# Moving the low-part differences of MoE1 from GpSimd to VectorE in an attention, MoE1, MoE2 kernel

## The chip, the cores and the metric

The kernel runs on one core of a Trainium2 chip. The metric is device time in microseconds (us), smaller is better. Engine names in the profile: PE is TensorE, PEld its weight load, DVE is VectorE, ACT is ScalarE, POOL is GpSimd, SP is SyncE, whose queue carries most loads. Each engine takes its own instructions in the order in which the program wrote them.

## The reference, cut to what matters

```
x = causal_attention(q, k, v)                    # 2 x 12 heads, 448 positions, head size 64
x -> 896 tokens x 768                            # heads laid side by side
h = x @ w_in                                     # 768 -> 2048
g = h * sigmoid(1.702 * h)
y = g @ w_out                                    # 2048 -> 768           (this is MoE1)
e = argmax(y @ w_gate); MoE2: relu(y @ w1[e]) @ w2[e], scaled by two gates
```

The weights w_in and w_out of MoE1 arrive as 64-bit floats; everything else is 32-bit.

## The kernel before, in words

**Split matmuls.** A 32-bit operand that is to be multiplied precisely is held as two numbers that TensorE takes at its fast rate: a high part (the value cast to the type `F32R` by ScalarE) and a low part (value minus high part). A product then takes three matmuls: high by high, high by low, low by high. So each weight and each activation costs a cast on ScalarE and then a subtraction that must wait for the cast.

**The stages.** Attention runs first (to about 138 us in the trace). Then L1 of MoE1 (x by w_in and the sigmoid gate, to 258.5 us), L2 of MoE1 in two passes (256 of the 768 output columns for seven token tiles, called B, to about 318 us, then the other 512, called A, to about 404 us), and then MoE2, expert by expert, to the end.

**Weights of MoE1, a stream.** `Stream` holds 48 weight tiles of 128x512 in the order of their use: 24 of w_in, 8 of w_out for part B and 16 for part A. Each is loaded by SyncE into a raw buffer and worked on in three steps, and `st.pump(n)` carries out n steps at the place in the program where it is called. Step one (L219, L221) and the first half of step two (L224) are VectorE's and turn 64-bit words into 32-bit ones; the second half of step two is ScalarE's cast into the slot (L226); step three is the subtraction (L228). A slot is one of 19 places in a ring, freed when its last matmul is issued, and the temporary 32-bit tile has two buffers.

**L1.** For each f of 16 blocks of 128 output features, the program issues six groups of matmuls (kk = 0 to 5), six matmuls in a group (two token groups times three products, L438). After each group it calls `st.pump(1)`, or `st.pump(2)` from f = 12 to f = 14, and nothing in f = 15. So two weights are converted in each f, and up to four in f = 12. The pumps in attention's stage have worked on eight weights but for the last step of the eighth, which falls in f = 0; so from f = 1 to f = 11 the six steps of an f are, in program order: step 1, 2, 3 of one weight, then 1, 2, 3 of the next. Behind them stand the four gate pieces of the block: a sigmoid by ScalarE (L536) and a product by VectorE (L537) each. The result of f sits in two banks of PSUM until the products have read it. Odd blocks take their banks from a set of four, even blocks from a set of three; so the second bank of an even block f is the bank that the first half of block f - 2 used, and its first matmul waits until the first two gate products of f - 2 are done. (PSUM tiles `ph0` and `ph4`, L431 to L433.)

**The first gate pieces of L2.** `gsplit(u)` (L496 to L509) casts a piece of g of 128x512 (ScalarE, L506) and subtracts (L508). 28 pieces serve pass B and 28 pass A. They are made three ahead of use and stand in four buffers, so that the cast of piece u + 3 waits for the matmuls of piece u - 1. For the 18 pieces listed in `GP` the subtraction is GpSimd's, for the other 38 VectorE's.

**L2, pass B.** A token tile t takes 16 values of kk, three matmuls each. At kk = 0, 4, 8 and 12 it calls `gsplit`, at kk = 5 it transposes the y of the tile before on TensorE and copies it out on VectorE (L618), at kk = 11 it multiplies that copy by the gate weights (L628), and after each kk it pumps `R2[t]` steps: 0.3 for t = 1, 2, 3 and 5, less for the others (0.1, 0.15, 0.2). TensorE's order is the program's order, so a copy L618 that is late holds every matmul behind L628.

Of the kernel before, what the change touches and what calls it, by code (L numbers as in the profile page):

```python
# [9 lines left out]
F32 = mybir.dt.float32  # L10
# [97 lines left out]
def kernel(ctx, tc, q, k, v, w_in, w_out, w_gate, w_og, w1, w2, out):  # L108
    nc = tc.nc
# [25 lines left out]
    CUT = 5  # L135
    NOV = 6
    XK = (11, 12, 13)
    GP = (4, 5, 7, 8, 10, 11, 13, 14, 16, 17, 19, 20, 22, 23, 25, 26, 27, 29)
    R1, R1B = 1, 2
    R2 = (0.1, 0.3, 0.3, 0.3, 0.15, 0.3, 0.2)  # L140
    R3 = (1.2, 1.2, 1.2, 1.2, 1.2, 1.2, 1.2)
# [17 lines left out]
    with tc.manual_schedule():  # L159
# [43 lines left out]
        def raw_tile(where, shape, dt):  # L203
            if where == "raw":
                return raws.tile(shape, dt, name="raw", tag="raw", bufs=RAW)
            return ringA.tile(shape, dt, name="rawA", tag=f"slotA{where}")

        def add64(keys, src, two=False, ring="A"):
            def load(where):
                raw = raw_tile(where, [128, 512], I64)  # L210
                nc.sync.dma_start(raw.rearrange("p (a n) -> p a n", a=2) if two else raw, src)
                return raw

            def work(keys, raw):
                slot = st.slots[keys[0]] = ring_slot(keys[0])
                r = raw.bitcast(U32).rearrange("p (n two) -> p n two", two=2)
                w = raws.tile([128, 512], F32, name="w32", tag="w32", bufs=2)
                wu = w.bitcast(U32)
                nc.vector.tensor_scalar(wu, r[:, :, 1], 3, 0x3FFFFFF8,  # L219
                                        op0=ALU.logical_shift_left, op1=ALU.bitwise_and)  # L220
                nc.vector.scalar_tensor_tensor(wu, r[:, :, 1], 0xC0000000, wu,  # L221
                                               op0=ALU.bitwise_and, op1=ALU.bitwise_or)
                yield
                nc.vector.scalar_tensor_tensor(wu, r[:, :, 0], 29, wu,  # L224
                                               op0=ALU.logical_shift_right, op1=ALU.bitwise_or)
                nc.scalar.copy(slot[:, 0], w)  # L226
                yield
                nc.gpsimd.tensor_sub(slot[:, 1], w, slot[:, 0].bitcast(F32))  # L228

            st.add(keys, ring, load, work)  # L230

# [2 lines left out]
        def ring_slot(key):  # L234
            ring, place = st.home[key]
            if ring == "A":
                return ringA.tile([128, 2, 512], F32R, name="slotA", tag=f"slotA{place}")
            return xr_p[0].tile([128, 2, 512], F32R, name="slotX", tag=f"slotX{place}")
# [83 lines left out]
        eng = {"D": nc.vector, "P": nc.gpsimd}  # L322
# [136 lines left out]
        for s in range(len(steps) + LAG + AV_AT[-1]):  # L459
# [12 lines left out]
            for c in range(NKC):  # L472
                u = s - LAG - (NQ - 1) - AV_AT[c]
# [22 lines left out]
        def gsplit(u):  # L496
            gnext[0] = u + 1
            if u >= 8 * TT:
                return
            t, qt = u % (4 * TT) // 4, u % 4  # L500
            if u < 2:
                gs = raws.tile([128, 2, GU, 128], F32R, name="gs0", tag="raw", bufs=RAW)
            else:
                gs = ggp.tile([128, 2, GU, 128], F32R, name="gs", tag="gs", bufs=4)
            src = g[t // 2 * 2][:, t % 2, GU * qt:GU * qt + GU, :]
            nc.scalar.copy(gs[:, 0], src)  # L506
            eng = nc.gpsimd if u in GP else nc.vector
            eng.tensor_sub(gs[:, 1], src, gs[:, 0].bitcast(F32))  # L508
            gsp[u] = gs  # L509

        for fq in range(4):
            for fc in range(4):
# [20 lines left out]
                for t0, nt in GT:  # L533
                    gv = g[t0][:, :, f, :]
                    pv = ph_t[f][t0 // 4].rearrange("q (t n) -> q t n", n=128)[:, t0 % 4:t0 % 4 + nt]
                    nc.scalar.activation(gv, pv, AF.Sigmoid, scale=1.702)  # L536
                    nc.vector.tensor_mul(gv, pv, gv)  # L537
                    if f == 15 and t0 == 0:
                        for u in range(2, 4):
                            gsplit(u)  # L540
                if fq == 3 and fc == 2:
                    assert st.nraw + 2 <= RAW
                    st.raws = RAW - 2
                    gsplit(0)
                    gsplit(1)
# [466 lines left out]
```

## Time and profile before

| what | value |
|---|---|
| time, median of 3 runs | 646.16 us (644.27 to 646.68) |
| the profiled execution's own time | 647.17 us |
| its span | 645.4 us |
| PE busy | 609.5 us, 94% of the span |
| DVE busy | 471.6 us, 73% |
| ACT busy | 373.6 us, 58% |
| POOL busy | 202.0 us, 31% |

The span is what the trace covers; the own time of that execution is 1.8 us more. Busy times are sums over instructions. An engine that is mostly busy over the whole run can still be idle for a long time in one stage, so the stages have to be looked at one by one.

### The profile page before, as it was taken

What the parts mean: (1) busy time and instruction counts of PE and PEld (TensorE: products, weight loads), DVE (VectorE), ACT (ScalarE), POOL (GpSimd) and SP (SyncE); (2) the same over time, 40 slices, a digit from 0 to 9 for tenths busy, and PEclk for the clock granted to TensorE, in tenths of its full rate; (3) what the DMA queues carried; (4) which work ended last, traced back from release to release, by engine and by line L of the source; (5) the groups of instructions that cost most, each with busy time, mean ns of one, the idle gap of its engine ahead of it and who ended that gap; (6) DMA issues with size and microseconds to landing.
All of it is one profiled execution on the core that took longest, in us unless ns stands there. A gap on an engine that the chain in (4) does not pass through costs nothing. (4 is left out here: it accounts for less than half of the span.)

```text
span 645.4 us, 10420 instructions
## 1 busy us (share of the span) xinstructions
PE 609.5 (94%) x3494; PEld 469.3 (73%) x3494; DVE 471.6 (73%) x890; ACT 373.6 (58%) x729; POOL 202.0 (31%) x291
## 2 busy tenths in 40 slices
PE   8999999999999979878999999959999999999995
PEld 4444544478888868867777777647888888888884
DVE  2766666637777777877855447757998888988896
ACT  4777777633333333434333224547888888888885
POOL 3344444416333342567511001241361110111110
PEclk8999999999999998999899999989999999999998
DMA  6735353115444453322393502446999999999960
GB/s 143 230 79 140 74 122 89 36 34 137 131 131 134 136 167 118 117 71 63 102 315 110 164 17 74 147 142 216 353 337 364 372 306 384 382 382 382 383 213 20
DMA packets 93146, 118.06 MB, mean 183 GB/s; under 512 B 40206, under 2 KB 53406, under 8 KB 93088
## 3 DMA queue, kind: packets, MB, share of 16 engines
q1 hardware_dynamic: 88560, 109.05, 52.2%
q0 software_dynamic: 2512, 5.54, 2.4%
q10 hardware_dynamic: 2016, 2.75, 1.2%
q8 instruction: 30, 0.49, 0.3%
q14 instruction: 28, 0.23, 0.1%
HBM read 114.10 MB, written 7.54 MB: 188 GB/s over the span
## 5 line engine op out<-in xcount | busy, mean ns | idle before, releaser
L576 PE MATMUL py<-slotA,gs 128*128 128x256 f32 (+1 forms) x609 | 115.1, 343 | 1.3 <-POOL gs L508 1.3
L576 PEld LDWEIGHTS py<-slotA,gs 128*128 128x128 f32 x609 | 93.5, 196 | 14.0 <-issue 2.6
L438 PE MATMUL ph<-xhi,slotA 128*128 128x512 f32 (+1 forms) x384 | 97.0, 372 | 4.7 <-DVE g L537 4.7
L228 POOL TENSOR_TENSOR slotA<-w,slotA 128x512 fp32r<-128x512 f32 x45 | 62.0, 1378 | 81.7 <-ACT slotA L226 81.6
L438 PEld LDWEIGHTS ph<-xhi,slotA 128*128 128x128 f32 x384 | 70.4, 190 | 15.2 <-issue 5.7
L226 ACT CAST slotA<-w 128x512 fp32r<-128x512 f32 x45 | 27.9, 620 | 89.2 <-DVE w L224 89.2
L301 DVE TENSOR_TENSOR ent<-wraw,ent 128x1024 fp32r<-128x1024 f32 x48 | 58.0, 1221 | 4.8 <-ACT ent L300 4.8
L367 PE MATMUL sc<-kz,qT 128*64 128x64 f32 (+6 forms) x336 | 56.3, 412 | 0.9 <-ACT kz L357 0.9
L380 DVE TENSOR_REDUCE nmax<-sc 128x1 f32<-128x64 f32 (+6 forms) x84 | 35.5, 422 | 29.6 <-PE sc L369 29.2
L391 POOL TENSOR_SCALAR P<-P,rc 128x64 f32<-128x64 f32 (+2 forms) x72 | 36.5, 508 | 65.4 <-DVE rc L390 56.3
L382 ACT ACTIVATE P<-sc,nmax 128x64 f32<-128x64 f32 (+6 forms) x84 | 40.0, 476 | 28.0 <-DVE nmax L380 15.9
L438 PE MATMUL ph<-xlo,slotA 128*128 128x512 f32 x192 | 56.0, 372 | 0.0
L508 DVE TENSOR_TENSOR gs<-g,gs 128x512 fp32r<-128x512 f32 x38 | 31.5, 836 | 31.9 <-ACT gs L506 31.8
L876 PE MATMUL ps_h<-ent,xh 128*128 128x512 f32 x192 | 53.8, 402 | 0.0
L224 DVE SCALAR_TENSOR_TENSOR w<-raw,w 128x512 uint32<-128x512 uint32 x46 | 51.9, 1129 | 1.2
L300 ACT CAST ent<-wraw 128x1024 fp32r<-128x1024 f32 x48 | 49.8, 1049 | 0.4 <-ACT y L598 0.4
L537 DVE TENSOR_TENSOR g<-ph,g 128x256 f32<-128x256 f32 x64 | 23.6, 389 | 29.6 <-ACT g L536 29.6
L506 ACT CAST gs<-g 128x512 fp32r<-128x512 f32 x56 | 33.1, 616 | 14.6 <-PE py L576 9.0
L876 PEld LDWEIGHTS ps_h<-ent,xh 128*128 128x128 f32 x192 | 35.0, 188 | 7.3
L301 DVE TENSOR_TENSOR ent<-wrb,ent 128x1024 fp32r<-128x1024 f32 x30 | 36.3, 1222 | 4.7 <-ACT ent L300 4.2
L221 DVE SCALAR_TENSOR_TENSOR w<-raw,w 128x512 uint32<-128x512 uint32 x46 | 38.0, 827 | 1.6
L438 PEld LDWEIGHTS ph<-xlo,slotA 128*128 128x128 f32 x192 | 35.5, 191 | 4.8
(190 smaller groups left out, 1202.4 us busy)
## 6 DMA issues: line engine op xcount, KB each, us to landing
wraw<-in_moe_w_dram SPq DMA_DIRECT2D x66, 512.0 KB, 7.7
wrb<-in_moe_w_dram SPq DMA_DIRECT2D x48, 512.0 KB, 9.0
wr<-in_moe_w_dram SPq DMA_DIRECT2D x30, 512.0 KB, 6.3
raw<-in_moe_w_in_dram SPq DMA_DIRECT2D x24, 512.0 KB, 4.5
raw<-in_moe_w_out_dram SPq DMA_DIRECT2D x22, 512.0 KB, 3.6
qraw<-in_q_dram SPq DMA_DIRECT2D x24, 112.0 KB, 2.9
kraw<-in_k_dram SPq DMA_DIRECT2D x24, 112.0 KB, 3.0
vraw<-in_v_dram SPq DMA_DIRECT2D x24, 96.0 KB, 2.6
```

Of the source, the lines that this page charges most:

```text
L221: nc.vector.scalar_tensor_tensor(wu, r[:, :, 1], 0xC0000000, wu, op0=ALU.bitwise_and, op1=ALU.bitwise_or)
L224: nc.vector.scalar_tensor_tensor(wu, r[:, :, 0], 29, wu, op0=ALU.logical_shift_right, op1=ALU.bitwise_or)
L228: nc.gpsimd.tensor_sub(slot[:, 1], w, slot[:, 0].bitcast(F32))
L300: nc.scalar.copy(hi, raw)
L301: nc.vector.tensor_sub(lo, raw, hi.bitcast(F32))
L367: nc.tensor.matmul(sc[64 * h:64 * h + 64, :n], qT[:, j * QB:(j + 1) * QB], kT[:, h, :n], start=True, stop=False)
L380: nc.vector.tensor_reduce(nm, sc[:, :n], axis=AX.X, op=ALU.max, negate=True)
L382: nc.scalar.activation(Pb[j][:, :n], sc[:, :n], AF.Exp, bias=nm, scale=1.0, accum_out=sm)
L391: eng[NORM_ENG[j]].tensor_scalar(Pb[j][:, :n], Pb[j][:, :n], rc, 1.0, op0=ALU.mult, op1=ALU.mult)
L438: nc.tensor.matmul(p[:, 0:128 * nt], wt, xt[:, kk, 128 * t0:128 * (t0 + nt)], start=kk == 0 and n == 0, stop=kk == KD - 1 and n == 2)
L576: nc.tensor.matmul(py[:, :n], gt[:, kk % 4], wt, start=kk == 0 and m == 0, stop=kk == KF - 1 and m == 2)
L876: nc.tensor.matmul(hps[hf], xh[:, k0 + n], wt[:, n], start=k0 + n == 0 and m == 0, stop=False)
```

## The change

Both subtractions that GpSimd did in MoE1 go to VectorE: step three of each weight (48 instructions, L228), and the 18 pieces of g in `GP` (L508). Their places in the program order stay the same.

```diff
-    GP = (4, 5, 7, 8, 10, 11, 13, 14, 16, 17, 19, 20, 22, 23, 25, 26, 27, 29)
...
                 nc.scalar.copy(slot[:, 0], w)
                 yield
-                nc.gpsimd.tensor_sub(slot[:, 1], w, slot[:, 0].bitcast(F32))
+                nc.vector.tensor_sub(slot[:, 1], w, slot[:, 0].bitcast(F32))
...
             nc.scalar.copy(gs[:, 0], src)
-            eng = nc.gpsimd if u in GP else nc.vector
-            eng.tensor_sub(gs[:, 1], src, gs[:, 0].bitcast(F32))
+            nc.vector.tensor_sub(gs[:, 1], src, gs[:, 0].bitcast(F32))
```

## Rows read from the trace of the kernel before

**Rows 1.** The page's busy times: us (share of the span) xinstructions.
```profile
PE 609.5 (94%) x3494; PEld 469.3 (73%) x3494; DVE 471.6 (73%) x890; ACT 373.6 (58%) x729; POOL 202.0 (31%) x291
```

**Rows 2.** Stretches: us, PE, PEld, DVE, ACT, POOL busy (count), PEclk, DMA share, GB/s.
```profile
75.00:100.00 25.00, 25.00 (x188) 12.08 (x184) 16.64 (x59) 18.18 (x57) 10.35 (x21) 1.00 0.45 107
140.50:222.50 82.00, 82.00 (x398) 72.18 (x397) 60.38 (x106) 27.29 (x65) 32.45 (x64) 1.00 0.44 130
258.50:318.70 60.20, 50.11 (x380) 46.74 (x380) 47.61 (x54) 24.94 (x50) 40.70 (x28) 0.94 0.28 87
294.70:301.20 6.50, 6.50 (x56) 6.17 (x54) 5.04 (x7) 3.17 (x6) 3.98 (x4) 1.00 0.35 101
```

**Rows 3.** Timeline of PE in L1: start us, us, instruction [idle before <-releaser].
```profile
230.58 0.99 PE L438 MATMUL ph<-xhi,slotA 128*128 128x512 f32 x4
231.82 0.99 PE L438 MATMUL ph<-xhi,slotA 128*128 128x512 f32 x4
...
242.27 0.64 PE L438 MATMUL ph<-xhi,slotA 128*128 128x384 f32 x1 [4.68 <-DVE g L537]
```

**Rows 4.** Timeline of DVE over one block f of L1.
```profile
182.90 0.42 DVE L219 TENSOR_SCALAR w<-raw 128x512 uint32<-128x512 uint32 x1
183.35 0.69 DVE L221 SCALAR_TENSOR_TENSOR w<-raw,w 128x512 uint32<-128x512 uint32 x1
184.08 0.69 DVE L224 SCALAR_TENSOR_TENSOR w<-raw,w 128x512 uint32<-128x512 uint32 x1
184.69 0.42 DVE L219 TENSOR_SCALAR w<-raw 128x512 uint32<-128x512 uint32 x1
...
185.87 1.66 DVE L224 SCALAR_TENSOR_TENSOR w<-raw,w 128x512 uint32<-128x512 uint32 x1
188.50 0.42 DVE L537 TENSOR_TENSOR g<-ph,g 128x256 f32<-128x256 f32 x1 [0.97 <-ACT g L536]
...
190.68 0.42 DVE L219 TENSOR_SCALAR w<-raw 128x512 uint32<-128x512 uint32 x1
```

**Rows 5.** Timeline of ACT in the same block.
```profile
184.80 0.62 ACT L226 CAST slotA<-w 128x512 fp32r<-128x512 f32 x1 [2.15 <-DVE w L224]
...
188.09 0.38 ACT L536 ACTIVATE g<-ph 128x256 f32<-128x256 f32 x1
```

**Rows 6.** Timeline of POOL in the same block.
```profile
185.50 1.48 POOL L228 TENSOR_TENSOR slotA<-w,slotA 128x512 fp32r<-128x512 f32 x1 [3.73 <-ACT slotA L226]
```

**Rows 7.** Instructions of L228, then of L508: duration ns min/median/max, first and last start.
```profile
L228 POOL TENSOR_TENSOR slotA<-w,slotA x45: 1261/1293/1747, 33.0 to 325.3; 128x512 fp32r<-128x512 f32 x45
...
L508 DVE TENSOR_TENSOR gs<-g,gs x38: 673/692/1726, 256.2 to 393.2; 128x512 fp32r<-128x512 f32 x38
```

**Rows 8.** Timeline of DVE: the first gate product of f = 0, 11, 12.
```profile
142.24 0.42 DVE L537 TENSOR_TENSOR g<-ph,g 128x256 f32<-128x256 f32 x1 [3.04 <-ACT g L536]
...
227.51 0.42 DVE L537 TENSOR_TENSOR g<-ph,g 128x256 f32<-128x256 f32 x1 [1.02 <-ACT g L536]
...
240.83 0.42 DVE L537 TENSOR_TENSOR g<-ph,g 128x256 f32<-128x256 f32 x1 [1.02 <-ACT g L536]
```

**Rows 9.** What PE waited for from 260 to 330 us: us, times, longest.
```profile
PE ps_lT L628 <- DVE yT L618: 7.9, 4, 3.7
PE py L576 <- POOL gs L508: 1.3, 1, 1.3
```

**Rows 10.** DVE's groups by form from 260 to 330 us: busy us, mean ns | idle before.
```profile
L508 DVE TENSOR_TENSOR gs<-g,gs 128x512 fp32r<-128x512 f32 x15 | 15.7, 1061 | 12.6 <-ACT gs L506 12.5
L224 DVE SCALAR_TENSOR_TENSOR w<-raw,w 128x512 uint32<-128x512 uint32 x9 | 11.9, 1323 | 0.2
L221 DVE SCALAR_TENSOR_TENSOR w<-raw,w 128x512 uint32<-128x512 uint32 x9 | 11.1, 1237 | 0.3
...
L618 DVE COPY yT<-ps_yT 128x256 f32<-128x256 f32 x7 | 2.9, 414 | 0.0
```

**Rows 11.** Timeline of DVE in pass B: a piece of g behind a weight's cast.
```profile
267.10 0.69 DVE L508 TENSOR_TENSOR gs<-g,gs 128x512 fp32r<-128x512 f32 x1 [1.26 <-ACT gs L506]
```

## The prediction, made before the changed kernel was run

> **What bounds the kernel now.** I read the page's busy times first [rows 1]: PE is busy for 94% of the span, so at most some 36 us of it are gaps, and a change of two other engines acts through those gaps or not at all. Next the busy times by stretch [rows 2]. In attention PE has no gap while DVE works 16.64 of 25 us. In L1 (140.5 to 222.5) PE is again busy throughout, DVE for 60.4 of 82 us. Pass B of L2 is the stage with holes: PE 50.1 of 60.2 us, at a granted clock of 0.94, against a tile without stalls, which takes 6.5 us.
>
> Then the timelines. They show that L1's full PE row hides a debt. A group of six matmuls takes 1.24 us [rows 3], so PE needs 6 x 1.24 = 7.44 us for a block f. DVE's round for the same block takes 190.68 - 182.90 = 7.78 us [rows 4], because DVE and ACT answer each other without slack in it. DVE falls behind by a third of a us in each block; PSUM covers that up to f = 14, whose second bank waits 4.68 us for the gate products of f = 12 [rows 3, 8]. So in L1 the chain DVE - ACT - DVE is already the slower one. In pass B PE's waits are 7.9 us for DVE's copy of y, and 1.3 us for POOL's pieces of g [rows 9].
>
> **The change, part by part: L1.** The subtraction takes POOL 1.29 us. On DVE the same shape, done there already for g, takes 0.69 us [rows 7], and DVE's next instruction begins 0.61 us after the start of one of 0.69 [rows 4]. What matters is that the subtraction now stands in DVE's own queue behind ACT's cast. Behind it in that queue are the next weight's L219, L221 and L224, and after the second weight the gate products, which free PSUM for PE. Step by step for one weight [rows 4, 5]: L219 to L221 0.45, L221 to L224 0.73, L224 itself 0.69, to the cast 0.03 (184.77 to 184.80), the cast 0.62, to the subtraction 0.03 (an ACT to DVE step is 0.03 at 188.47 to 188.50), the subtraction 0.61: together 3.16 us. Two weights take 6.32 us. Today they take 188.50 - 182.90 = 5.60. The gate pieces after them stay at 190.68 - 188.50 = 2.18 us: the first sigmoid, at 188.09, is ready before DVE is free in the new order too. The round becomes 8.50 us against PE's 7.44.
>
> A gain is already in that sum. Today the second L224 takes 1.66 us and the first 0.69 [rows 4], because POOL's subtraction runs from 185.50 to 186.98 [rows 6] and L224 ends 0.55 us after it; that 0.97 us goes away. So in DVE's own time a block grows by only 2 x 0.61 - 0.97 = 0.25 us. The rest is waiting: 2 x 0.68 for the casts, less the 0.97 that DVE waits today ahead of the gate products, 0.39, and 0.08 of overlap that is lost where an instruction is waited for to its end.
>
> [...]
>
> Where it ends. The first gate product of f = 0 stays at 142.24; that of f = 11 comes at 142.24 + 11 x 8.50 = 235.7 instead of 227.51 [rows 8]. In f = 12 four weights stand between: 2.18 + 4 x 3.16 = 14.8 instead of 13.3, so f = 12's comes at 250.6 instead of 240.83. PE's matmul follows 1.44 us later (240.83 to 242.27), at 252.0: **9.7 us late**. The debt is paid in parts, because even blocks wait for the products of f - 2: about 1.7 us ahead of f = 8 (PE there at 192.9, released at 142.24 + 6 x 8.50 + 1.44 = 194.7), 2.1 each ahead of f = 10 and 12, and 8.5 ahead of f = 14. From there PE has two blocks to do, and DVE's work of f = 13 (three weights, 9.5 us) and f = 14 ends before them. Bounds: if the casts were always done when DVE comes, 11 x 0.25 - 0.5 (f = 12: 4 x 0.61 less three stretched L224) = +2.3; with POOL's step from the cast of 0.08 (185.42 to 185.50) instead of 0.03, 26 x 0.05 more, +11.0. I take 9.7: the steps are read from one and the same queue.
>
> **Pass B.** DVE gets 29 more subtractions (11 weights, nine of them in rows 10 and two from other buffers, and 18 pieces of g), and its own instructions get shorter: L224 and L221 now average 1.32 and 1.24 us here and L508 1.06 [rows 10], against 0.69 where POOL is silent. A tile with rate 0.3 (four of seven) then holds 4 pieces x 0.61, 1.6 weights x (0.45 + 0.73 + 0.61 + 0.61), and two copies, some 0.5 (0.41 for the larger [rows 10]): 6.8 us. A piece of g that comes right behind an L224 waits for two casts on ACT, 1.26 us today [rows 11]; that should meet four weights in five, 1.3 a tile: 1.6 us. So 8.4 us a tile, for PE too, since the copy of y is in that queue. The three others hold 0.5 to 1.1 weights, 4.2 to 5.5 us, and run at PE's 6.5 us. 4 x 8.4 + 3 x 6.5 = 53.1, and with the first matmuls of pass A that the stretch contains and an uneven start some 55.5 instead of 60.2: **4.7 us gained**. Bounds: all that is lost there today, 60.2 - 7 x 6.5 = 14.7 us gained; or DVE's 29 x 0.69 = 20.0 us more with only its 12.6 idle us [rows 10] to take them, 7.4 us lost. I stay nearer to the first kind because the row 1.66 against 0.69 says that most of what DVE gives here is time that it lost.
>
> **Attention** takes eight subtractions. They are emitted a pump after the cast, and DVE is idle for 8 of 25 us under a PE without gaps [rows 2]: nothing. Uncovered they would be 8 x 0.69 = 5.5 us; below nothing there is no room, as PE has no gap. The constants on POOL and pass A, whose pieces are DVE's today, lie beside other work. The loads follow freed buffers, so they move with PE and pay nothing back later.
>
> **Sum.** 647.17 (this execution's own time, 645.4 of it span) + 9.7 - 4.7 = 652.2. The median of the runs is 1.0 lower. I give 652, on the upper side, because longer gaps in L1 may lower the clock once more as those of pass B do (0.94).
>
> **The rivals.**
> *It cancels.* L1 as above, but pass B gains 8 to 10 because without POOL its copies of y are never late. For it: 7.9 of PE's waits there end with that copy [rows 9]. Against it: DVE's 6.8 us in a heavy tile exceed PE's 6.5 even without a wait. 646 to 649.
> *Faster, because DVE is no longer stretched.* If DVE came to the subtraction after the cast was done (the third steps standing behind the gate products instead of ahead of them, which would also mean that the change is not what the step count says), L1 would lose 2.3 only, and pass B gain 9 to 14.7: 634.8 to 640.5. It decides once pass B gains more than L1 loses. For it: the stretched durations of rows 10. Against it: the order of the steps, by which the cast always starts after the L224 just ahead. [...]
> *Slower still.* In pass B every weight and every piece of g waits for ACT and DVE becomes the bound in all tiles: 647.2 + 9.7 + 7.4 = 664.3. For it: ACT's casts hold 12.5 us of DVE's idle time there [rows 10]; against it: three tiles have room.
>
> **How the numbers follow.** Forecast 0.60, cancelling 0.17, faster 0.08, slower still 0.15 (between the forecast and 664). A difference of 0.5%, 3.2 us, is about what can be told from none; so slower means above 649.4 and faster below 642.9. Slower 0.75 (the forecast and the last rival), same 0.17, faster 0.08. The range 646.5 to 660 leaves out the fast rival and the upper half of the slow one.
>
> **What would show it.** In L1, DVE rounds of 8.5 us with every L224 at 0.69 and an idle 0.7 ahead of each L228; waits of PE ahead of f = 8, 10, 12 of about 2 us each and of some 8.5 ahead of f = 14; L2 starting near 268 instead of 258.5. In pass B, L221, L224 and L508 at 0.69 and a stage of some 55.5 us, with L618 still ending waits. The prediction is wrong if L1's rounds stay under 8 us, or if pass B doesn't shorten, or shortens by more than L1 grows.

## The result, and the profile after

The kernel after takes 653.21 us (median of 4 runs, 651.99 to 653.40) against 646.22 for the one before beside it (644.27 to 646.68): ratio 1.011, with a 95% interval of 1.0086 to 1.0134. The forecast was 652, slower. The profiled execution took 653.3 us (span 651.3), 6.1 us more than the one of before. Line numbers of after are one less than before up to the cast of a piece of g (now L505) and two less from its subtraction (now L506) on.

The page's busy times of after, in the columns of [rows 1]:

```profile
PE 607.1 (93%) x3494; PEld 467.0 (72%) x3494; DVE 474.8 (73%) x956; ACT 373.8 (57%) x729; POOL 108.9 (17%) x225
```

DVE has 66 instructions more and is busy for only 3.2 us more, though 66 steps of 0.61 us from one subtraction to the next instruction are 40 us: nearly all that it took over it had been losing while POOL worked beside it. By this page alone the change looks free. The stages say where it isn't. I divide each span at three matmuls of PE's timeline: the last but one group of attention's output products (L417, L416 in after; the last group stands among products of L1), the first `py` product, which opens L2, and the first transpose of y that pass A issues. All stage lengths below are taken in the same way.

| us | before | after | difference |
|---|---|---|---|
| up to that attention group | 133.06 | 131.53 | -1.53 |
| L1 | 125.44 | 137.28 | +11.84 |
| pass B | 60.12 | 56.26 | -3.86 |
| the rest | 326.78 | 326.23 | -0.55 |
| span | 645.40 | 651.30 | +5.90 |

The first row is no gain of the change: from the score products (L367) at 29.21 us before and 27.81 after to that group attention takes 103.85 us before and 103.72 after. The other 1.4 us lie in the start of the span, ahead of any weight's subtraction. The same score products start at 10.04 us in both and take 1.66 us before, where the granted clock from 9 to 13 us is 0.65, and 0.97 after, where it is 1.00; profiles of other kernels below have either start. The row of before, then that of after:

```profile
10.04 1.66 PE L367 MATMUL sc<-kz,qT 128*64 128x448 f32 x4
10.04 0.97 PE L366 MATMUL sc<-kz,qT 128*64 128x448 f32 x4
```

PE's timeline of after in L1, the rows that wait, and the first product of L2 (the one of before has the row of 242.27 in [rows 3] and no other):

```profile
193.61 0.41 PE L437 MATMUL ph<-xhi,slotA 128*128 128x384 f32 x1 [1.90 <-DVE g L535]
210.62 0.41 PE L437 MATMUL ph<-xhi,slotA 128*128 128x384 f32 x1 [1.91 <-DVE g L535]
227.75 0.41 PE L437 MATMUL ph<-xhi,slotA 128*128 128x384 f32 x1 [2.25 <-DVE g L535]
251.42 0.66 PE L437 MATMUL ph<-xhi,slotA 128*128 128x384 f32 x1 [8.56 <-DVE g L535]
...
268.81 1.36 PE L574 MATMUL py<-slotA,gs 128*128 128x256 f32 x10
```

The first product of L2 in before:

```profile
258.50 8.07 PE L576 MATMUL py<-slotA,gs 128*128 128x256 f32 x66
```

One wait has become four, ahead of f = 8, 10, 12 and 14, 14.6 us instead of 4.7. DVE's timeline over one block f = 5 shows who makes them; read it against [rows 4]:

```profile
177.33 0.42 DVE L218 TENSOR_SCALAR w<-raw 128x512 uint32<-128x512 uint32 x1
177.78 0.69 DVE L220 SCALAR_TENSOR_TENSOR w<-raw,w 128x512 uint32<-128x512 uint32 x1
178.51 0.69 DVE L223 SCALAR_TENSOR_TENSOR w<-raw,w 128x512 uint32<-128x512 uint32 x1
179.89 0.69 DVE L227 TENSOR_TENSOR slotA<-w,slotA 128x512 fp32r<-128x512 f32 x1 [0.69 <-ACT slotA L225]
180.50 0.42 DVE L218 TENSOR_SCALAR w<-raw 128x512 uint32<-128x512 uint32 x1
...
183.06 0.69 DVE L227 TENSOR_TENSOR slotA<-w,slotA 128x512 fp32r<-128x512 f32 x1 [0.69 <-ACT slotA L225]
183.67 0.42 DVE L535 TENSOR_TENSOR g<-ph,g 128x256 f32<-128x256 f32 x1
...
185.84 0.42 DVE L218 TENSOR_SCALAR w<-raw 128x512 uint32<-128x512 uint32 x1
```

Ahead of each L227 DVE stands idle for 0.69 us until ACT's cast of the same weight is done, and the gate products L535, which PE needs, stand behind it. The round is 185.84 - 177.33 = 8.51 us instead of 7.78, PE's own 7.44. No L223 is stretched any more.

The stretches of after, in the columns of [rows 2]: the same 25 us of attention, the two parts of L1 behind the last wait, and pass B.

```profile
75.00:100.00 25.00, 25.00 (x186) 12.18 (x185) 18.25 (x63) 18.12 (x56) 8.34 (x19) 1.00 0.50 117
251.40:258.10 6.70, 6.68 (x20) 5.93 (x21) 4.74 (x10) 1.52 (x3) 0.00 (x0) 0.55 0.28 89
258.10:268.80 10.70, 10.70 (x53) 9.42 (x52) 7.13 (x15) 4.08 (x11) 0.00 (x0) 1.00 0.31 98
268.80:325.10 56.30, 48.62 (x380) 45.28 (x380) 43.08 (x81) 25.16 (x50) 0.75 (x1) 0.97 0.30 94
```

In attention DVE has 1.6 us more to do and PE still no gap. After the wait of 8.56 us PE works without a gap at a granted clock of 0.55 for 6.7 us, and then at 1.00. In before the same stretch behind the wait of 4.68 is 4.0 us long, at 0.57:

```profile
242.30:246.30 4.00, 4.00 (x12) 3.57 (x13) 3.52 (x8) 0.90 (x2) 0.64 (x1) 0.57 0.17 52
```

DVE's groups of after in pass B (268 to 335 us, busy us, mean ns | idle before), against [rows 10]:

```profile
L506 DVE TENSOR_TENSOR gs<-g,gs 128x512 fp32r<-128x512 f32 x33 | 22.4, 686 | 11.5 <-ACT gs L505 10.9 <-PE py L574 0.5
L220 DVE SCALAR_TENSOR_TENSOR w<-raw,w 128x512 uint32<-128x512 uint32 x9 | 6.2, 693 | 0.3
L223 DVE SCALAR_TENSOR_TENSOR w<-raw,w 128x512 uint32<-128x512 uint32 x9 | 6.2, 684 | 0.0
L227 DVE TENSOR_TENSOR slotA<-w,slotA 128x512 fp32r<-128x512 f32 x8 | 5.5, 686 | 1.9 <-ACT slotA L225 1.9
```

Nothing is stretched: the means fell from 1061, 1237 and 1323 ns to between 684 and 693. And what PE waited for there (268 to 340 us: us, times, longest), against [rows 9]:

```profile
PE ps_lT L626 <- DVE yT L616: 5.1, 5, 1.8
PE ps_lT L626 <- issue: 1.8, 1, 1.8
```

The copy of y is still what ends PE's waits, 5.1 us instead of 7.9, with 1.8 more that the profile puts down to nothing; the wait for POOL's pieces is gone. Of the 3.9 us by which pass B is shorter, PE's gaps give 2.4 (10.1 to 7.7 us) and PE's busy time gives 1.5 (50.11 to 48.62 us, at a clock of 0.97 instead of 0.94).

### The profile page after: what moved, and what is told of

Same layout as the page of the kernel before. It is cut to its first block, busy times and chain, and to the rows that moved or that the text cites. A ratio compares the mean times of both kernels' runs of the same rounds, so it can differ in the third digit from the quotient of the medians.

```text
span 651.3 us, 10352 instructions
## 1 busy us (share of the span) xinstructions
PE 607.1 (93%) x3494; PEld 467.0 (72%) x3494; DVE 474.8 (73%) x956; ACT 373.8 (57%) x729; POOL 108.9 (17%) x225
## 5 line engine op out<-in xcount | busy, mean ns | idle before, releaser
L574 PE MATMUL py<-slotA,gs 128*128 128x256 f32 (+1 forms) x609 | 113.5, 340 | 0.0
L437 PE MATMUL ph<-xhi,slotA 128*128 128x512 f32 (+1 forms) x384 | 98.7, 375 | 14.7 <-DVE g L535 14.6
L574 PEld LDWEIGHTS py<-slotA,gs 128*128 128x128 f32 x609 | 92.0, 193 | 12.5 <-issue 2.3
L506 DVE TENSOR_TENSOR gs<-g,gs 128x512 fp32r<-128x512 f32 x56 | 38.2, 688 | 30.5 <-ACT gs L505 29.9
L437 PE MATMUL ph<-xlo,slotA 128*128 128x512 f32 x192 | 56.3, 374 | 0.0
L390 POOL TENSOR_SCALAR P<-P,rc 128x64 f32<-128x64 f32 (+2 forms) x72 | 37.9, 527 | 71.7 <-DVE rc L389 63.0
L227 DVE TENSOR_TENSOR slotA<-w,slotA 128x512 fp32r<-128x512 f32 x45 | 31.0, 689 | 22.4 <-ACT slotA L225 22.4
L505 ACT CAST gs<-g 128x512 fp32r<-128x512 f32 x56 | 33.2, 617 | 13.9 <-PE py L574 8.2
L398 PE MATMUL ps_pT<-ident,P 128*128 128x128 f32 x192 | 37.4, 288 | 0.0
L535 DVE TENSOR_TENSOR g<-ph,g 128x256 f32<-128x256 f32 x64 | 23.5, 387 | 16.4 <-ACT g L534 16.1
L534 ACT ACTIVATE g<-ph 128x256 f32<-128x256 f32 x64 | 21.0, 355 | 22.8 <-DVE g L535 20.9
```

Source lines behind the costliest of these rows:

```text
L390: eng[NORM_ENG[j]].tensor_scalar(Pb[j][:, :n], Pb[j][:, :n], rc, 1.0, op0=ALU.mult, op1=ALU.mult)
L398: nc.tensor.transpose(ps[:, c].rearrange("p h q -> p (h q)"), Pb[j][:, c * KC:(c + 1) * KC], ident)
L437: nc.tensor.matmul(p[:, 0:128 * nt], wt, xt[:, kk, 128 * t0:128 * (t0 + nt)], start=kk == 0 and n == 0, stop=kk == KD - 1 and n == 2)
L506: nc.vector.tensor_sub(gs[:, 1], src, gs[:, 0].bitcast(F32))
L574: nc.tensor.matmul(py[:, :n], gt[:, kk % 4], wt, start=kk == 0 and m == 0, stop=kk == KF - 1 and m == 2)
```

## Experiments

Two explanations of the loss stand against each other. Mine: the subtraction stands **in the wrong place of DVE's queue**, behind ACT's cast and ahead of the gate products, so that DVE waits 0.69 us for each weight. The rival: DVE simply has **too much to do** with all 66 subtractions, wherever they stand. A third statement is about the gain in pass B: it comes from DVE and POOL no longer holding each other up. The table has all kernels that were timed more than once, e5_both's one run stands in its paragraph; kernels on the same chip share the runs of before. The stage lengths are of the one profiled execution.

| kernel | us | before beside it | ratio, 95% | L1 | pass B |
|---|---|---|---|---|---|
| before | | | | 125.4 | 60.1 |
| after | 653.21 | 646.22 | 1.0110 (1.0086 to 1.0134) | 137.3 | 56.3 |
| e1_weights | 655.75 | 645.50 | 1.0174 (1.0129 to 1.0219) | 136.8 | 58.9 |
| e2_pieces | 642.07 | 645.50 | 0.9941 (0.9919 to 0.9963) | 126.3 | 56.6 |
| e3_l2only | 641.70 | 645.50 | 0.9939 (0.9915 to 0.9963) | 126.3 | 55.6 |
| e4_late | 647.72 | 645.50 | 1.0034 (1.0014 to 1.0055) | 125.2 | 59.3 |
| e6_slow_pump | 657.36 | 644.72 | 1.0189 (1.0146 to 1.0231) | 131.8 | 59.0 |
| e7_logits15 | 639.69 | 644.72 | 0.9918 (0.9885 to 0.9951) | 125.2 | 54.2 |
| e8_behind | 635.08 | 645.21 | 0.9850 (0.9825 to 0.9874) | 119.0 | 56.4 |
| e9_behind15 | 633.91 | 645.21 | 0.9823 (0.9797 to 0.9850) | 119.0 | 54.6 |
| e10_shift | 650.52 | 645.21 | 1.0074 (1.0048 to 1.0100) | 134.6 | 55.8 |

**e1_weights: the weights alone.** The kernel before, with only this line changed:

```diff
-                nc.gpsimd.tensor_sub(slot[:, 1], w, slot[:, 0].bitcast(F32))
+                nc.vector.tensor_sub(slot[:, 1], w, slot[:, 0].bitcast(F32))
```

> Only the weights' subtractions (48) move to VectorE; the 18 pieces of g stay on GpSimd. Theory (the loss is made in L1, by a subtraction that stands in VectorE's queue behind ScalarE's cast and ahead of the gate products): L1 as with the whole change, rounds of 8.5 us, PE waits for gate products of 14 to 15 us instead of 4.7. Pass B keeps GpSimd's pieces, so VectorE is still stretched there: 58 to 62 us against 60.2 before and 56.3 after. In all 655 to 660. Rival (what counts is how much VectorE has to do in all): 48 of 66 subtractions, so some three quarters of the change's +7, about 651.

10.3 us slower. L1 is as long as in after, so the weights alone make its loss. PE's waits there are shorter than I expected, 11.4 us in four; what they lack went into the clock. The stretch behind the first wait (1.91 us, ahead of 193.7):

```profile
193.70:210.70 17.00, 16.61 (x72) 14.32 (x72) 12.40 (x25) 4.92 (x12) 0.00 (x0) 0.90 0.43 123
```

PE is busy for 16.61 us at 0.90 here. In after it is busy for 15.10 us at 1.00 in the same 17 us and waits for the rest:

```profile
193.60:210.60 17.00, 15.10 (x72) 13.01 (x73) 12.40 (x25) 4.93 (x12) 0.00 (x0) 1.00 0.40 122
```

DVE's rounds are 8.51 us in both. PE arrives when DVE lets it, by waiting or by working slowly: the length is set by DVE's round.

**e2_pieces: the pieces of g alone.** The kernel before, with the list `GP` not used:

```diff
-            eng = nc.gpsimd if u in GP else nc.vector
-            eng.tensor_sub(gs[:, 1], src, gs[:, 0].bitcast(F32))
+            nc.vector.tensor_sub(gs[:, 1], src, gs[:, 0].bitcast(F32))
```

> Only the 18 pieces of g move; the weights' subtractions stay on GpSimd. Theory: L1 as before (rounds of 7.78 us, one wait of PE of 4.7 us), pass B shorter than before because neither engine holds the other up for the pieces: 54 to 58 us. In all 641 to 644. Rival (VectorE's load): a quarter of the change's loss, about 648.

3.4 us faster, with L1's single wait of before (4.72). The two halves add up: +10.3 - 3.4 = +6.9 against after's +7.0. So the pieces are the good half of the change and the weights the bad one.

**e3_l2only: the weights on POOL up to the end of L1, on DVE from pass B on.**

```diff
-                nc.vector.tensor_sub(slot[:, 1], w, slot[:, 0].bitcast(F32))
+                low[0].tensor_sub(slot[:, 1], w, slot[:, 0].bitcast(F32))
...
+        low = [nc.gpsimd]
...
         st.limit = RAW
+        low[0] = nc.vector
```

> The whole change, but the weights' subtractions that are emitted in L1 (and attention) stay on GpSimd; those of pass B and A and all pieces of g are VectorE's. Theory: L1 as before with 4.7 us of waits, pass B as with the whole change, 56 us: before minus 4, so 641 to 643. Rival (pass B is short after the change only because PE comes to it later, with weights further ahead): pass B stays near 60 us and the time near 646.

3.8 us faster than before. L1 keeps one wait (4.76), pass B has after's order without its clock loss (1.00 against 0.97) and takes 55.6 us. All that after loses, it loses by the subtractions that stand ahead of pass B.

**e4_late: the subtraction behind the next weight's first steps, everywhere.** All stay on DVE; each is issued after the next weight's L218 and L220 (or before its first use).

```diff
                                                op0=ALU.bitwise_and, op1=ALU.bitwise_or)
+                flush()
                 yield
...
-                nc.vector.tensor_sub(slot[:, 1], w, slot[:, 0].bitcast(F32))
+                late.append((keys, lambda: nc.vector.tensor_sub(slot[:, 1], w, slot[:, 0].bitcast(F32))))
```

> All 66 subtractions on VectorE, but a weight's subtraction is written behind the first step of the next weight (after its L219 and L221, which do not wait for the cast), so the cast runs beside VectorE's work. Same instructions and same engines as the whole change. Theory: VectorE never waits for a weight's cast; a block's round is 2 x (0.45 + 0.61 + 0.61 + 0.61) less what the second subtraction moves behind the gate products, plus 0.97 for cast and sigmoid: about 7.8 us as before, f = 12 about 12.4 instead of 13.3. PE's waits in L1 3 to 5 us, pass B 52 to 56 us; in all 638 to 643. Rival (VectorE's added 0.61 us each is the cost, wherever it stands): rounds of 8.5 us and 653 as with the whole change.

L1 did what the first explanation says: rounds of 7.77 us, one wait (4.44), 125.2 us, 12 less than after with the same load on DVE. The total was a miss. Attention grew by 1.4 us (103.85 to 105.28), and pass B took 59.3 us where I had expected 52 to 56, because three of its tiles ran at a lower clock: PE is busy for 51.73 us there, at 0.91, against 48.62 in after, and its gaps are as long (7.6 and 7.7 us). One of them, PE's timeline of e4_late:

```profile
270.86 0.41 PE L639 MATMUL ps_lT<-yT,wg 128*32 128x128 f32 x4 [1.83 <-issue]
271.20 5.35 PE L587 MATMUL py<-slotA,gs 128*128 128x256 f32 x30
```

and the same two groups in a tile of after:

```profile
306.39 0.41 PE L626 MATMUL ps_lT<-yT,wg 128*32 128x128 f32 x4 [1.82 <-DVE yT L616]
306.73 3.86 PE L574 MATMUL py<-slotA,gs 128*128 128x256 f32 x30
```

Thirty equal products take 5.35 us after one wait of 1.83 and 3.86 after another of 1.82. The granted clock is 0.67 from 271.2 to 276.4 in e4_late, and 1.00 from 306.4 to 310.6 in after.

**e5_both: POOL does each weight's subtraction too**, in L1, into a tile that nobody reads; DVE does it as in after. This measures what the two engines cost each other.

```diff
+                if scr:
+                    nc.gpsimd.tensor_sub(scr[0], w, slot[:, 0].bitcast(F32))
                 nc.vector.tensor_sub(slot[:, 1], w, slot[:, 0].bitcast(F32))
```

> The whole change, and in L1 GpSimd does each weight's subtraction as well, into a scratch tile that nobody reads; VectorE's program is untouched. Theory (the engines hold each other up when both read two inputs): VectorE's instructions beside GpSimd's are stretched again, 0.69 to some 1.3 to 1.7 us once or twice a weight, a block's round grows from 8.5 to 9.5 to 11 us, PE's waits in L1 from 14.6 to 25 to 45 us, and the time from 653 to 664 to 685. Rival (the 1.66 us of before had another cause, such as the order of the work): no VectorE instruction over 0.75 us in L1, rounds of 8.5, time 653.

668.97 us in one run (before beside it 644.72), with six waits of PE in L1, 26.8 us together, and rounds of 9.6 us. DVE's timeline there:

```profile
165.53 0.69 DVE L229 TENSOR_TENSOR slotA<-w,slotA 128x512 fp32r<-128x512 f32 x1 [0.69 <-ACT slotA L225]
166.14 1.51 DVE L218 TENSOR_SCALAR w<-raw 128x512 uint32<-128x512 uint32 x1
```

and POOL's:

```profile
165.64 1.73 POOL L228 TENSOR_TENSOR scr<-w,slotA 128x512 f32<-128x512 f32 x1 [3.62 <-ACT slotA L225]
```

DVE's subtraction starts 0.11 us ahead of POOL's and keeps its 0.69; POOL's takes 1.73 instead of 1.29 [rows 7]; and the L218 behind it takes 1.51 instead of 0.42, to 0.28 us after POOL's end at 167.37. Behind the second subtraction of a block stand the gate products, which read one of their inputs from PSUM, and beside POOL's second subtraction they keep their 0.42. DVE's row, then POOL's:

```profile
170.40 0.42 DVE L542 TENSOR_TENSOR g<-ph,g 128x256 f32<-128x256 f32 x1
```

```profile
169.90 1.74 POOL L228 TENSOR_TENSOR scr<-w,slotA 128x512 f32<-128x512 f32 x1 [2.54 <-ACT slotA L225]
```

So the overlap costs DVE 1.09 us once in a block, and that is what the round grows by (8.51 to 9.60). Why L218 grows beside POOL and the gate products don't, no row here shows. The third statement isn't tested as directly, since no run adds POOL's work in pass B alone; there the rows show that DVE does 27 instructions more in 4.5 us less (54 in 47.61 us before [rows 2], 81 in 43.08 after).

**e6_slow_pump: one step of the stream for each group in f = 12 to 14 too** (`R1, R1B = 1, 1` instead of 1, 2), so that two weights and not four stand ahead of f = 12's gate products.

> The whole change, with one step a group also in f = 12 to 14 (R1B = 1 instead of 2): two weights in each of these blocks instead of four and three, six in all instead of seven. Theory (the four weights of f = 12, each with its wait for the cast, make the wait of 8.6 us ahead of f = 14): f = 12's round 8.6 instead of 15, PE's wait ahead of f = 14 falls to about 2 us; DVE then still has two weights in f = 14 ahead of the last gate products, so L1 ends 4 to 6 us earlier, and one weight more falls into L2: 647 to 651. Rival (the debt is only moved, since DVE's sum of work is the same): 653.

L1 did as expected: waits of 1.91, 2.14, 2.02 and 2.36 us, without the one of 8.6, and 5.5 us less than after. The 131.8 us even hold a new wait of 3.41 us ahead of the first product of L2, for ACT's cast of a piece of g (L505). But the kernel got slower, against the forecast: the steps that L1 leaves undone come due later. Pass B took 59.0 us, and in pass A PE waited for a weight:

```profile
335.83 0.49 PE L574 MATMUL py<-slotA,gs 128*128 128x512 f32 x1 [1.71 <-ACT slotA L225]
337.68 3.48 PE L574 MATMUL py<-slotA,gs 128*128 128x512 f32 x8 [1.35 <-DVE slotA L227]
```

With the double pump, which makes the wait of 8.56 us in L1, after has none of these.

**e7_logits15: a later use of the copy of y.** e3_l2only, with pass B's gate products (L628 of before) at kk = 15 instead of 11:

```diff
-                hooks[11] = lambda t=t: logits(t - 1, "B")
+                hooks[15] = lambda t=t: logits(t - 1, "B")
```

> As the run with the weights of L1 left on GpSimd and all else on VectorE (641.7), and in pass B the gate matmuls stand at kk = 15 instead of kk = 11, so that the copy of y has ten groups instead of six before PE needs it. Theory A (in pass B PE waits because one copy is late in VectorE's queue, which has the room): pass B falls from 55.6 to 48 to 51 us, time 635 to 638. Theory B (VectorE's sum of work and waits for casts is what bounds pass B, 8 us a tile): PE then waits for the pieces of g or for the later copy instead, pass B 53 to 56 us, time 640 to 643.

639.69 us, pass B 54.2 at a clock of 1.00. Up to 330 us the wait for the copy of y fell from e3_l2only's 7.7 us to 3.7, and the wait of the transposes for ACT's y grew from 0.8 to 3.7: the chain between PE, ACT and DVE around y holds what is left. In the total the gain over e3_l2only isn't clear of the noise (the intervals overlap).

**e8_behind: the test between the two explanations.** e4_late's order in L1 only; and one more step of the stream in f = 0, so that the gate products of each block stand behind a subtraction whose cast is done by then. All 66 subtractions are DVE's, as in after.

```diff
+                late.append((keys, lambda: nc.vector.tensor_sub(slot[:, 1], w, slot[:, 0].bitcast(F32))))
+                if not defer[0]:
+                    flush()
...
+        defer[0] = True
         for fq in range(4):
...
+                if f == 0:
+                    st.pump(1)
```

> All 66 subtractions on VectorE. In L1 a weight's subtraction is written behind the next weight's first step, and the pump is moved on by one step, so that the gate pieces of a block follow a first step and not a cast. Theory (position in the queue, not VectorE's load): rounds of 2 x 2.28 + 2.18 = 6.7 us of work, so VectorE waits for PE's 7.44; four weights in f = 12 take 11.3 us and the wait ahead of f = 14 goes away. PE's waits in L1 0 to 2 us, L1 some 119 to 121 us long against 125.4 before and 137.3 after the change; pass B 56 us; time 634 to 638. Rival (load): L1 no shorter than before, time 646 or more.

635.08 us: the same instructions on the same engine as in after, and 10 us less than the before beside it, where after takes 7 more. DVE's timeline of e8_behind in L1, over a bit more than one block:

```profile
204.57 0.69 DVE L224 SCALAR_TENSOR_TENSOR w<-raw,w 128x512 uint32<-128x512 uint32 x1
205.17 0.42 DVE L218 TENSOR_SCALAR w<-raw 128x512 uint32<-128x512 uint32 x1
205.62 0.69 DVE L220 SCALAR_TENSOR_TENSOR w<-raw,w 128x512 uint32<-128x512 uint32 x1
206.24 0.68 DVE L228 TENSOR_TENSOR slotA<-w,slotA 128x512 fp32r<-128x512 f32 x1
207.56 0.42 DVE L554 TENSOR_TENSOR g<-ph,g 128x256 f32<-128x256 f32 x1 [0.64 <-ACT g L553]
...
215.00 0.42 DVE L554 TENSOR_TENSOR g<-ph,g 128x256 f32<-128x256 f32 x1 [0.64 <-ACT g L553]
```

L218 and L220 of the next weight now lie between L224 and the subtraction L228, and no L228 of L1 waits: its cast ran beside them. The round is 215.00 - 207.56 = 7.44 us, PE's own, so the debt that even the kernel before ran up is gone. The stretch of all of L1:

```profile
132.70:251.80 119.10, 119.06 (x581) 103.59 (x582) 89.10 (x180) 41.13 (x95) 1.77 (x21) 1.00 0.45 134
```

PE is busy for 119.06 of 119.10 us at a clock of 1.00, with DVE at 89.10 us busy. The rival falls: with this load DVE still has 30 us to spare in L1.

**e10_shift: the extra step in f = 0 without the new order.** After with only the last two lines of the diff above.

> The whole change with the pump moved on by one step alone; each subtraction still stands right behind its cast. Theory (the wait for the cast is half of the cost): two waits of 0.7 us stay in each block, the round is still 2 x 3.16 + 2.18 = 8.5 us, PE's waits in L1 12 to 15 us, time 650 to 654. Rival (only the place ahead of the gate products costs): rounds of 7.5 us, PE's waits below 5 us, time 640 to 644.

650.52 us, rounds of 8.39 us and four waits of 13.5 us together, L1 134.6. So L1 was measured in all four ways: 137.3 us in after, 134.6 with the shift alone, 125.2 with the new order alone (e4_late), 119.0 with both. The new order gives 12 us by itself and 15.5 on top of the shift; the shift gives 2.7 us by itself, of which 1.3 lie in the clock behind the last wait (16.09 us from the release to the first product of L2, 17.39 in after), and 6.2 on top of the order.

**e9_behind15: e8_behind with e7_logits15's line.**

> As the run before it, with the gate matmuls of pass B at kk = 15. If L1's gain and the later gate matmuls add: 2 us less than that run, 632 to 636. If pass B is bound by VectorE's and ScalarE's sum there, no difference.

633.91 us, pass B 54.6 instead of 56.4: the version with the lowest median. Its runs reach from 632.12 to 636.99 and overlap e8's, so that the last us isn't settled.

## Why the prediction was right, step by step

- **Round and wait for the cast: right.** 8.51 us measured, 8.50 predicted; 0.69 idle ahead of each subtraction, 0.7 predicted; L223 at 0.69 throughout.
- **Where the debt is paid: right.** Waits of 1.90, 1.91, 2.25 and 8.56 us against 1.7, 2.1, 2.1 and 8.5.
- **The sum for L1: too small by 2.1 us** (9.7 predicted, 11.84 measured). One half is the chain of gate products. From f = 0's to f = 12's it took 249.99 - 140.69 = 109.30 us, and 108.4 were predicted (250.6 - 142.24): the first round, where f = 0's gate pieces took 2.61 instead of 2.18 us, and the last three, 8.62, 8.62 and 15.06 instead of 8.50, 8.50 and 14.82. The other half is the clock, which I had named and given no price but the rounding up from 651.2 to 652: from the release by f = 12's products to the first product of L2 PE needs 268.81 - 251.42 = 17.39 us, and needed 258.50 - 242.27 = 16.23 before. This isn't the price of the longer wait: the same stretch took 16.09 us behind e10_shift's wait of 8.34 and 17.03 behind e2_pieces' of 4.72. What sets it stays open, so this half may be chance.

After's timeline of DVE, where the first of these numbers is read:

```profile
140.69 0.42 DVE L535 TENSOR_TENSOR g<-ph,g 128x256 f32<-128x256 f32 x1 [2.43 <-ACT g L534]
...
249.99 0.42 DVE L535 TENSOR_TENSOR g<-ph,g 128x256 f32<-128x256 f32 x1
```

- **Pass B: right in kind, 0.8 us short** (4.7 predicted, 3.9 measured). A heavy tile was to take 8.4 us: from one group of gate products to the next PE takes 8.47, 8.33, 8.39 and 8.33 us. The lighter tile between them took 7.09, not 6.5. One tile again ran at a lower clock (0.70 from 281.2 to 286.9 us, thirty products in 5.20 us).
- **Attention at nothing: right**, 103.72 us against 103.85 (with seven subtractions there, the last at 122.4 us, and not eight). e4_late shows what it costs when the order there changes: 1.4 us.
- **The rivals.** That it cancels fell, as pass B's copies of y are still late. That it gets faster fell for this order, but its condition was right: where the cast is done when DVE comes (e8_behind), L1 loses nothing and the kernel takes 635 us, at the low end of the 634.8 to 640.5 given for it. That the total fits is luck: pass B gained 3.7, not the 9 to 14.7 of that sum. And I had put L1 at a loss of 2.3 even then; it gained 6.4, because the same order also ends the debt that the kernel before runs up (rounds of 7.44 us instead of 7.78). That pass B gets slower fell.
- The profiled execution came out 1.1 us above the sum (653.3 against 652.2) and the median 1.2 above the forecast, partly by luck: the sum missed by +2.1 in L1 and +0.8 in pass B, less 1.5 for the start of the span and 0.6 for the rest. Without these two, of which the first is no work of the change, it would have been some 3 us above.

## What to carry to other kernels

When an instruction moves to another engine, write down that engine's queue with it in place and ask what it waits for there and what stands behind it; busy shares do not show this (DVE's rose by 3.2 us in a kernel that lost 7). A step that follows another engine's result belongs behind the next independent work of its own engine: the same 66 instructions cost 7 us in one place and gave 10 in the other, with one step of the stream moved. And where two parts of a change act in different stages, time them apart, since here one was worth -3.4 us and the other +10.3.

## What the runs showed of the hardware

**The clock after waits of PE isn't settled.** In pass B waits of 1.83 (after, e4_late) and 1.76 us (e4_late) were followed by thirty products in 5.20, 5.35 and 5.35 us, and waits of 1.82 and 1.77 (after, e3_l2only) by 3.86 and 3.85. In L1 a wait of 1.91 us was followed by a clock of 0.90 in e1_weights and of 1.00 in after. Behind four waits of over 4 us in L1 the clock was 0.54 to 0.57 each time, but not for longer behind the longer ones: 4.0 us at 0.57 behind 4.68 (before) and 6.7 at 0.55 behind 8.56 (after), shown above, but some 3.5 at 0.56 behind 8.34 (e10_shift, first row) and some 5.7 at 0.54 behind 4.72 (e2_pieces, second row).

```profile
250.00:253.50 3.50, 3.47 (x10) 3.13 (x11) 2.38 (x6) 0.90 (x2) 0.00 (x0) 0.56 0.21 43
240.70:246.40 5.70, 5.65 (x16) 5.05 (x17) 5.22 (x9) 1.10 (x3) 1.42 (x1) 0.54 0.39 121
```

The length of the wait alone decides neither, and no run here shows what does; e4_late's 59.3 us in pass B have this part open.

**L218, an instruction of VectorE with one input, takes longer beside POOL too.** I had looked for this only in those with two inputs. L218 has one input of 128x512, runs in 0.42 us where those with two of that size take 0.69, and took 1.51 beside POOL in e5_both; in the kernel before the same instruction (L219) takes up to 1.50. In e5_both it ends 0.28 us behind POOL's end instead of ahead of it, and POOL's subtraction, which started 0.11 us after DVE's, grew from 1.29 to 1.73 us. Through what the two engines hold each other up, no run here shows.
